# Windowed attention with sinks and a mixing feed-forward layer: rows of two tokens throughout, and a new order of work

## Chip, cores and metric

The kernel runs on one core of a Trainium2 chip. The metric is the device time of one execution in microseconds. Runs come with a state: "fast" runs agree with the fastest of the same kernel within 1.5%, "slow" ones do not and are left out of every ratio. In the kernel before, TensorE's granted clock is 0.98 as a mean over the profiled run.

## The reference, cut to what matters

```python
def _attn_ref(q, k, v, n_sink, window):          # (4, 8, 768, 64) each, n_sink 4, window 128
    scores = scale * np.matmul(q, k.transpose(0, 1, 3, 2))
    keep = is_sink | in_window                   # the first 4 tokens, and the last 128
    a = softmax(np.where(keep, scores, -1e9))    # cut: written out with max, exp, sum
    return np.matmul(a, v)

def _moe_ref(x, mu_k, mu_r, w_k, w_v, w_r):      # x is (4, 768, 512)
    x_prev = ...                                 # x, one token later
    xk = mu_k * x + (1.0 - mu_k) * x_prev
    xr = mu_r * x + (1.0 - mu_r) * x_prev
    k = np.maximum(xk @ w_k, 0.0)                # "keys"
    v = k * k @ w_v                              # "v products"
    r = 1.0 / (1.0 + np.exp(-(xr @ w_r)))        # "gates"
    return r * v
```

## The kernel before: the parts concerned

The work is cut into 12 units of 256 tokens (4 batches, T = 0, 1, 2 in each). A table in the kernel fixes which engine does each movable operation (CHOICE) and the order on each engine (ORDER). Buffers come from pools, and waits follow from what an operation reads and writes. A unit passes through: load; cast to bf16; transpose (on TensorE and evacuated, or by DMA); scores; exponential; mask; values; transpose of x; mix; keys; v products and gates. In the profile lines, `xt` is transposed x, `xk` and `xr` are the mixed x, `rl` the keys after their maximum with 0, `kk` their square, `th` the gates, `ob` an output block, `e` the exponentials, `es` those of the sinks, and `vb` the v rows in bf16.

```python
# evacuation of transposed q and k: pairs of tokens are pulled apart (strided)
copy(out=buf[key][:, 2 * half:2 * half + 2, :, :].rearrange("p c g (t j) -> p c j (g t)", j=2),
     in_=buf[psk].bitcast(BF16)[:, 0:512].rearrange("p (c j t) -> p c j t", c=2, j=2))
...
def scores(c):                                   # 6 products per head pair, 4 of them where T == 0
    jobs = [(kt[:, c, 0, :], 128, 384, qt[:, c, :, :]),
            (kt[:, c, 1, :], 384, 512, qt[:, c, 1, :])]
    if T > 0:
        jobs.append((buf["kt", u - 1][:, c, 1, :], 0, 128, qt[:, c, 0, :]))
...
# mix, for each half of the 512 columns: one subtraction, then a fused multiply-add for each
# of two 128-column blocks and each of xk and xr
nc.vector.tensor_tensor(out=buf[tk], in0=xt[:, c0:c0 + 2, t0:t0 + 256],
                        in1=xt[:, c0:c0 + 2, t0 - 1:t0 + 255], op=ALU.subtract)
nc.vector.scalar_tensor_tensor(
    out=buf[key][:, c0 + i, :], in0=buf[tk][:, i, :],
    scalar=mu[w][:, c0 + i:c0 + i + 1],
    in1=xt[:, c0 + i, t0 - 1:t0 + 255], op0=ALU.mult, op1=ALU.add)
```

The softmax here doesn't subtract the row's maximum and nothing guards it: scores larger than these inputs give would overflow.

## Time and profile before

| | before |
|---|---|
| time, median of 3 runs | 171.59 us (170.52 to 173.14) |
| span of the profiled run | 169.6 us |
| busy TensorE / VectorE / ScalarE / GpSimd | 160.0 / 153.4 / 129.0 / 13.5 us |
| TensorE work, at the smallest spacing of each product | 143.6 us |

The last row is not a row of the page. It is worked out from the trace: each weight load is counted at its start with the spacing of its product as the prediction lists them (216 ns for 512 columns, 109 for 256, and so on; score groups spread over their products). The same count up to a time t says how much TensorE had done by then. I call it "work done".

Beside the lines in the prediction, these are the busy times in three stretches of the kernel before (columns: stretch, length, then busy time and count of PE, PEld, DVE, ACT and POOL, granted clock, DMA share, GB/s; PE is TensorE and PEld its weight loads, DVE is VectorE, ACT ScalarE, POOL GpSimd):

```profile
0.00:30.00 30.00, 24.58 (x231) 15.55 (x231) 23.12 (x66) 21.93 (x34) 5.96 (x22) 0.89 0.97 262
30.00:130.00 100.00, 99.01 (x1041) 66.10 (x1041) 99.26 (x261) 85.61 (x140) 7.51 (x9) 1.00 0.92 214
130.00:176.00 46.00, 36.42 (x335) 24.04 (x332) 31.02 (x78) 21.44 (x36) 0.00 (x0) 0.99 0.35 98
```

In the middle stretch TensorE and VectorE are both full and ScalarE has 14 us of 100 to spare. Over the whole span these shares look much looser (94, 90 and 76%).

### The profile page before, as it was taken

The page shows a single profiled execution, that of the slowest core. Times are in us where ns is not written, and L with a number is a line of the kernel's source. Part 1 is how long each engine was busy: PE and PEld are TensorE (multiplying, and loading weights), DVE is VectorE, ACT ScalarE, POOL GpSimd, SP SyncE. Part 2 cuts the span into 40 slices and gives each one's busy share as a digit, 9 for nine tenths or more (in the row PEclk, how much of TensorE's full clock was granted, in tenths as well). Part 3 has the DMA queues.
Part 4 walks back from the last instruction along what each step waited for, and adds up shares of the span by engine and source line. Part 5 has one row for each costly group of instructions (what it writes and reads, how often), then busy time and mean ns, then how long its engine had stood idle before and what let it go on. Part 6 is the DMA issues. An engine that isn't in the chain of part 4 may idle for free.

```text
span 169.6 us, 4184 instructions
## 1 busy us (share of the span) xinstructions
PE 160.0 (94%) x1602; PEld 105.7 (62%) x1602; DVE 153.4 (90%) x403; ACT 129.0 (76%) x208; POOL 13.5 (8%) x31
## 2 busy tenths in 40 slices
PE   7977879799999999999999999999999999999992
PEld 2544658664657667767567786756476775877551
DVE  6288898999999999999999999999999999799542
ACT  3588797999898999897979986866829849953320
POOL 6330000000200010050000200030000000000000
PEclk9995699999999999999999999999999999999999
DMA  5999989999938979999579489969969858103033
GB/s 142 238 275 320 344 192 326 356 335 276 191 86 214 254 172 231 184 263 287 135 183 221 97 207 225 181 168 233 252 147 266 195 109 233 62 4 124 2 124 124
DMA packets 82803, 33.82 MB, mean 199 GB/s; under 512 B 64736, under 2 KB 77280, under 8 KB 82784
## 3 DMA queue, kind: packets, MB, share of 16 engines
q1 hardware_dynamic: 81728, 33.56, 80.0%
q8 instruction: 12, 0.20, 0.5%
q10 hardware_dynamic: 1056, 0.00, 0.4%
q14 instruction: 7, 0.06, 0.1%
HBM read 24.12 MB, written 6.29 MB: 179 GB/s over the span
## 4 chain that ended last, share of the span: by engine, by line
PE 82%; DVE 10%; DMA 3%; SPq 1%; issue 1%; ACT 0%; POOL 0%; DVEq 0%
PE bank L888 24%; PE bank L839 23%; PE bank L870 12%; PE bank L713 7%; PE sc L654 6%; DMA vs<-in_v_dram 3%; PE bank L752 3%; PE bank L569 2%; PE bank L701 2%; DVE e L690 2%; DVE xk L789 2%; SPq L387 1%; DVE x L729 1%; PE bank L631 1%; PE bank L809 1%
## 5 line engine op out<-in xcount | busy, mean ns | idle before, releaser
L839 PE MATMUL bank<-xk,wk_sb 128*128 128x256 bf16 x384 | 50.5, 273 | 1.1 <-DVE wk_sb L513 0.9
L676 ACT ACTIVATE e<-sc 128x1024 bf16<-128x1024 f32 (+1 forms) x48 | 44.6, 966 | 4.4 <-PE sc L654 4.4
L888 PE MATMUL bank<-wv_h,kk 128*128 128x512 bf16 x184 | 45.8, 379 | 0.0
L839 PEld LDWEIGHTS <-wk_sb 128*128 128x128 bf16 x384 | 35.3, 98 | 9.3 <-DVE wk_sb L513 1.4
L849 ACT ACTIVATE rl<-bank 128x512 bf16<-128x512 f32 x45 | 26.2, 607 | 10.3 <-PE bank L839 7.8
L690 DVE TENSOR_TENSOR e<-e,mask 128x1024 bf16<-128x1024 bf16 (+1 forms) x48 | 30.1, 639 | 0.4 <-POOL ksink L608 0.3
L888 PEld LDWEIGHTS <-kk 128*128 128x128 bf16 x184 | 16.7, 98 | 15.7 <-issue 0.5
L870 PE MATMUL bank<-wr_sb,xr 128*128 128x512 bf16 x96 | 24.2, 379 | 0.0
L789 DVE SCALAR_TENSOR_TENSOR xk<-td,mu,xt 128x256 bf16<-128x256 bf16 x48 | 22.4, 493 | 0.1
L789 DVE SCALAR_TENSOR_TENSOR xr<-td,mu,xt 128x256 bf16<-128x256 bf16 x48 | 22.5, 477 | 0.0
L876 ACT ACTIVATE th<-bank 128x512 f32<-128x512 f32 x24 | 14.8, 620 | 7.8 <-PE bank L870 7.7
L729 DVE TENSOR_TENSOR x<-bank,rec 128x256 bf16<-128x256 f32 x48 | 19.4, 416 | 0.6 <-DVE rec L726 0.3
L897 DVE SCALAR_TENSOR_TENSOR ob<-th,bank 128x512 f32<-128x512 f32 x23 | 15.6, 681 | 4.7 <-ACT th L876 2.6
L861 DVE TENSOR_TENSOR kk<-rl 128x512 bf16<-128x512 bf16 x48 | 19.4, 416 | 0.1
L713 PE MATMUL bank<-vb,e 128*128 128x65 bf16 x352 | 19.2, 195 | 0.2
L713 PEld LDWEIGHTS <-e 128*128 128x128 bf16 x352 | 16.7, 99 | 3.1 <-issue 0.6
L654 PE MATMUL sc<-qt,kt 64*128 64x128 bf16 (+1 forms) x256 | 14.8, 247 | 1.1 <-ACT kt L577 0.7
L870 PEld LDWEIGHTS <-xr 128*128 128x128 bf16 x96 | 8.9, 98 | 8.6 <-issue 0.3
L654 PEld LDWEIGHTS <-kt 64*128 64x128 bf16 x256 | 9.5, 97 | 7.3 <-issue 4.0
L761 ACT COPY xt<-bank 128x512 bf16<-128x512 bf16 x15 | 8.8, 587 | 5.3 <-PE bank L752 4.5
L701 PE MATMUL bank<-vsink,es 128*128 128x130 bf16 x64 | 12.4, 220 | 0.3 <-ACT rl L849 0.3
L779 DVE TENSOR_TENSOR td<-xt 128x512 bf16<-128x512 bf16 x24 | 10.5, 440 | 0.1
(63 smaller groups left out, 163.9 us busy)
## 6 DMA issues: line engine op xcount, KB each, us to landing
vs<-in_v_dram SPq DMA_DIRECT2D x24, 256.0 KB, 4.6
out_dram<-ob SPq DMA_DIRECT2D x23, 256.0 KB, 3.3
ks<-in_k_dram SPq DMA_DIRECT2D x18, 256.0 KB, 4.8
qs<-in_q_dram SPq DMA_DIRECT2D x7, 512.0 KB, 7.3
qs<-in_q_dram SPq DMA_DIRECT2D x10, 256.0 KB, 5.3
w<-in_moe_w_k_dram SPq DMA_DIRECT2D x2, 1024.0 KB, 10.3
w<-in_moe_w_v_dram SPq DMA_DIRECT2D x2, 1024.0 KB, 10.0
ks<-in_k_dram SPq DMA_DIRECT2D x3, 512.0 KB, 8.2
```

What stands on the lines that cost most here:

```text
L654: nc.tensor.matmul(out=sc[:, a, o0:o1], lhsT=lhs[rows], rhs=rhs[rows], start=True, stop=True)
L676: nc.scalar.activation(out=buf[ek][:, :, lo:], in_=buf[sck][:, :, lo:], func=AF.Exp, scale=scale)
L690: nc.vector.tensor_tensor(out=at, in0=at, in1=m, op=ALU.mult)
L701: nc.tensor.matmul(out=o[:, g, :, :], lhsT=buf["es", u][:, 128 * g:128 * g + 128], rhs=vsink[b % 2][:, 2 * c:2 * c + 2, :], start=True, st ...
L713: nc.tensor.matmul(out=o[:, g, a, :], lhsT=e[:, a, e0:e0 + 128], rhs=rhs, start=(T == 0 and i == 0), stop=(i == len(blocks) - 1), skip_gro ...
L729: P.op("DVE", dve(256), lambda ok=ok, rk=rk, c=c: nc.vector.tensor_tensor(out=buf["x", u][:, :, 128 * c:128 * c + 128].rearrange("p g (a d ...
L789: nc.vector.scalar_tensor_tensor(out=buf[key][:, c0 + i, :], in0=buf[tk][:, i, :], scalar=mu[w][:, c0 + i:c0 + i + 1], in1=xt[:, c0 + i, t ...
L839: nc.tensor.matmul(out=ps[:, i, :], lhsT=wk_sb[:, c, 128 * f:128 * f + 128], rhs=xk[:, c, :], start=(c == 0), stop=(c == NC - 1), skip_gro ...
L849: nc.scalar.activation(out=buf[rk], in_=buf[psk].rearrange("p (i t) -> p i t", i=2), func=AF.Relu)
L861: P.op("DVE", dve(512, 0.52), lambda f2=f2, rk=rk: nc.vector.tensor_tensor(out=buf["kk", u][:, 2 * f2:2 * f2 + 2, :], in0=buf[rk], in1=buf ...
L870: nc.tensor.matmul(out=buf[psk], lhsT=buf["xr", u][:, c, 128 * g:128 * g + 128], rhs=wr_sb[:, c, :], start=(c == 0), stop=(c == NC - 1))
L888: nc.tensor.matmul(out=buf[psk], rhs=wv_h[:, f, :], lhsT=buf["kk", u][:, f, 128 * g:128 * g + 128], start=(f == 0), stop=(f == NF - 1))
```

## The change

Its intent: load q, k and v in rows of two consecutive tokens, so that DMA packets are 512 bytes rather than 256; keep tokens in that pair order everywhere, so that the evacuation of q and k is contiguous; move the mix from fused operations to two-source operations and scalings that may go to ScalarE, and some casts to GpSimd; mask the first two units by products added to the scores; and search CHOICE and ORDER anew. Cut to its core:

```diff
 # loads: v like q and k, "h (p j) d -> p h (j d)" with j=2 (two tokens, 512 bytes, in a row)
-                        in_=v[b, :, s0:s0 + 128, :].rearrange("h p d -> p h d")), rank,
+            key, src = (name, u), {"k": k, "q": q, "v": v}[name]
 # casts of q and k: a third engine is allowed
-                       "DVE": (dve(512, 0.52), cast(nc.vector.tensor_copy), True)},
+                       "DVE": (dve(512, 0.52), cast(nc.vector.tensor_copy), True),
+                       "POOL": (590.0, cast(nc.gpsimd.tensor_copy), True)},
 # evacuation: contiguous
-                    out=buf[key][:, 2 * half:2 * half + 2, :, :].rearrange(
-                        "p c g (t j) -> p c j (g t)", j=2),
+                    out=buf[key][:, 2 * half:2 * half + 2, :, :],
 # v rows of two neighbouring units joined (T > 0): two copies of 64 x 1040 per unit
+                P.op("DVE", 456.0, part(nc.vector.tensor_copy), rank, port=True,
+                     alts={"DVE": (456.0, part(nc.vector.tensor_copy), True),
+                           "ACT": (970.0, part(nc.scalar.copy), False)},
 # sinks' v rows: two products with a selection matrix
+            for j in range(2):
+                nc.tensor.matmul(..., lhsT=spread[0:NS // 2, j, :],
+                                 rhs=buf["vb", u][0:NS // 2, j, :, 0:D], start=(j == 0), stop=(j == 1))
 # scores: 8 products of 128 columns per head pair, for every T; exponentials always 1024 wide
+                            out=sc[:, a, :].rearrange("p (j g t) -> p j g t", j=2, g=2)[:, j, g],
+                            lhsT=kt[rows, c, j, at:at + 128], rhs=q2[rows, g],
 # mix: subtract (2 per unit), scale (8), add the shifted tokens (4)
-                        nc.vector.scalar_tensor_tensor(
-                            out=buf[key][:, c0 + i, :], in0=buf[tk][:, i, :],
-                            scalar=mu[w][:, c0 + i:c0 + i + 1],
-                            in1=xt[:, c0 + i, t0 - 1:t0 + 255], op0=ALU.mult, op1=ALU.add)
+                    nc.vector.tensor_scalar(
+                        out=buf[key][:, c, :], in0=buf[xr][:, c, :],
+                        scalar1=mu[w][:, c:c + 1], scalar2=None, op0=ALU.mult)
+                    nc.scalar.activation(out=buf[key][:, c, :], in_=buf[xr][:, c, :],   # or this
+                                         func=AF.Copy, scale=mu[w][:, c:c + 1])
+                    nc.vector.tensor_tensor(out=part, in0=part, in1=behind(g), op=ALU.add)
 # mu: loaded as 8 rows, transposed on TensorE, copied;  CHOICE and ORDER: all new
```

## The prediction

> **What bounds the kernel now.** I read, in this order: the busy table with the slices, the chain that ended last, busy times by window, the timeline of TensorE over the first 30 us, the cost groups by form.
>
> ```profile
> PE 160.0 (94%) x1602; PEld 105.7 (62%) x1602; DVE 153.4 (90%) x403; ACT 129.0 (76%) x208; POOL 13.5 (8%) x31
> ...
> PEclk9995699999999999999999999999999999999999
> ...
> PE 82%; DVE 10%; DMA 3%; SPq 1%; issue 1%; ACT 0%; POOL 0%; DVEq 0%
> ```
>
> TensorE is busy 94% and carries 82% of the chain. VectorE at 90% looks like a second bound, but the windows (columns: length, then busy time and count of PE, PEld, DVE, ACT, POOL, clock, DMA share, GB/s) separate two stages:
>
> ```profile
> 16.00:20.00 4.00, 3.68 (x37) 2.71 (x39) 3.15 (x9) 2.92 (x5) 0.00 (x0) 0.50 1.06 378
> 20.00:24.00 4.00, 2.35 (x20) 1.35 (x16) 4.00 (x10) 4.00 (x6) 0.00 (x0) 0.98 0.83 164
> ...
> 85.00:100.00 15.00, 15.00 (x172) 10.74 (x170) 15.00 (x41) 13.27 (x22) 1.17 (x1) 1.00 0.78 169
> ...
> 145.00:160.00 15.00, 15.00 (x143) 10.90 (x141) 13.24 (x35) 8.31 (x14) 0.00 (x0) 1.00 0.14 54
> ```
>
> After about 30 us TensorE has no holes. "Busy" is modelled, so I also took the spacing of single matmul starts in the trace: 216 ns for 512 columns, 109 for 256, 56 for 128, 29 for the 65-column value products. Everything above these spacings between 30 us and the last matmul (166.1 us) adds up to 3.1 us of 136. VectorE being full there is nearly free of charge. Before 30 us things differ: TensorE at half clock, then short of work while VectorE and ScalarE are full.
>
> ```profile
> 21.54 0.28 PE L631 MATMUL bank<-qt,ksink 128*32 128x256 bf16 x2 [0.79 <-DVE qt L577]
> 21.75 1.05 PE L839 MATMUL bank<-xk,wk_sb 128*128 128x256 bf16 x8
> 22.64 0.59 PE L908 MATMUL bank<-warm 128*128 128x512 bf16 x2
> 24.11 1.92 PE L839 MATMUL bank<-xk,wk_sb 128*128 128x256 bf16 x16 [0.87 <-DVE wk_sb L513]
> ```
>
> The first keys product starts at 21.75 and work is dense only from 24.1 us. From the spacings, all work that is not filling costs: keys 384 x 109 = 41.9 us, v products 184 x 216 + 16 x 109 = 41.4, gates 96 x 216 = 20.7, scores 16 x 0.55 + 8 x 0.44 = 12.3, values 352 x 29 + 64 x 57 = 13.9, transposes 192 x 56 = 10.8, sinks 2.6, sum 143.6 us, plus some 0.1 us at each of 32 switches into the narrower score shapes (a 512-column product before one takes 312, not 216 ns): 146.8 us. At 24.1 us only 6.9 us of it was done. So the time is a start-up of 24 us, a dense TensorE stage of 142, and 3.5 us of tail. Only the start-up and TensorE's own work count.
>
> **What the Trainium skill says.**
> "TensorE: Matmul & The Clock Gate", Part 1 (the HAM clock gate): the array runs at half rate unless it has recently been busy. The trace agrees: clock 0.50 at 16 to 20 us, after holes at 10 to 13, and 1.00 later.
> "VectorE: DVE Perf Modes", What auto-detection actually checks: a two-tensor operation can do two 16-bit results per cycle, a single-source one in SBUF more. The trace agrees for the first: kk (512 elements, two sources) takes 416 ns, while the fused scalar-tensor-tensor takes 477 to 493 for only 256, so it has no fast form here.
> "DMA: Bandwidth & Descriptors", Specifications: line rate wants 512 B or more. The DMA records agree: a 256 B packet takes 20 ns, a 512 B one 30.
> "GPSIMD Engine Reference", Specifications: its SBUF interfaces are shared with VectorE. GpSimd is idle 92% of this run, so this trace cannot show what that costs.
>
> **The change, part by part.** Counts of the changed kernel are from its instruction order.
>
> TensorE. Scores become 16 products of 128 columns per two head pairs for all tokens. Two products on separate row halves start 3 to 4 ns apart and pairs 56 ns apart, so 8 pairs cost about 0.55 us: unchanged where T > 0, +0.11 us for each of 8 groups at T = 0. Values: 352 becomes 384 products, 32 x 29 ns = +0.9 us. The sinks' v rows take two products, not one: 4 x 0.22 = +0.9. A quarter of these falls in the start-up; the dense stage gains about **2.0 us of work** (0.65 + 0.70 + 0.65). The masks of the first two units become 16 added bias products of 512 columns, 3.5 us, all before the first keys product, partly in place of fills (22 become 17).
>
> VectorE. Rows of the groups, mean ns of one at the bar:
>
> ```profile
> L690 DVE TENSOR_TENSOR e<-e,mask 128x1024 bf16<-128x1024 bf16 x32 | 21.3, 681 | 0.2 <-ACT e L676 0.2
> ...
> L779 DVE TENSOR_TENSOR td<-xt 128x512 bf16<-128x512 bf16 x24 | 10.5, 440 | 0.1
> ...
> L577 ACT COPY qt<-bank 128x512 bf16<-128x512 bf16 x11 | 8.3, 757 | 0.2 <-PE bank L569 0.2
> ...
> L591 ACT CAST vb<-vs 128x512 bf16<-128x512 f32 x13 | 8.3, 639 | 0.0
> ```
>
> The mix is 24 subtractions and 96 fused operations, 55.4 us; it becomes 72 two-source operations at 0.44 (31.7) and 45 scalings at an estimated 0.2 us (a four-element reciprocal takes 0.175) = 40.7, so -14.7. Masks: 48 become 40, 30.1 to 27.2. Casts -2.1, eight joins of v rows an estimated +3.6, five more relus +3.4, the rest +1.8. Sum about -11: 142 us.
>
> ScalarE. Evacuations of k and q become contiguous: 17 at 0.745 become 11 at the 0.587 of xt, -6.2. Casts -10.7. Scalings 51 x 0.38 (the 256-element es) = +19.4; eight joins at about 1.04 = +8.3; 16 exponentials grow from 768 to 1024 elements at 0.82 to 1.04, +3.5; others -5.3. Sum +9: 138 us. GpSimd takes 19 casts of q and k and more. Both of VectorE's and ScalarE's totals stay below TensorE's.
>
> DMA. 49,152 packets of 256 B become 24,576 of 512 B: 61.4 to 46.1 us of the 16 engines, share 80 to about 71%. After 40 us no TensorE wait ends on a DMA, so that is free; in the start-up v is 0.64 us per unit cheaper. The mu load (about 1000 packets of 4 B) nearly vanishes, but lies beside other loads.
>
> **Start-up**, where it is decided. ScalarE up to its first cast of wk: now 11.6 us of work from 4.6 us on, so 16.2, really 20.25 (4 us of waits). Then: 6 casts at 0.57, 5 evacuations at 0.55, 2 joins at 1.0, 8 exponentials at 0.97, es and two scalings 1.05: 17.0 us, so 21.6 without waits, and keys from 22.7. VectorE loses eight masks (4.7 us), which made such waits; I allow 1 us and put keys at 23.7. But by then both first units' values and two groups of the third's scores are done, some 8.1 us in the units of before; at 24.1 us that is 8.5 against 6.9: **-1.6 us**. A looser VectorE should save half of the roughly 4 us that were lost after 24 us: **-1.5 to -2**. Against it **+2.0**. If the clock stays up at 13 to 20 us, the chain's TensorE pieces there (3.5 us at half speed) give another 1 us or so. Sum -1 to -3, middle **-2 us**.
>
> **The rivals.**
> A: the start-up gains much more. The new order puts no fill after the first unit's scores, as if TensorE were then always supplied; if so it is dense from about 11 us with 2 us done: 11 + 2.6 of bias + 145 left + 2.8 of switches + 3.5 = 165 us of span, time about 166.5. Against: 17 us of ScalarE work and a DMA share above 1 ahead of wk. The same sort of order in the kernel before lost far more than it planned.
> B: ScalarE becomes the start-up's bound and wk's casts come at 24 to 25 us, or keys of the second unit, which follow at once, wait for its longer mix (subtract, scale, add over two engines, xt still to be evacuated). Then the 2 us of added products come on top: 172 to 173.5.
> C: GpSimd's 20 to 30 us of casts hold VectorE at the shared interface and eat the 11 us. It costs the time only if VectorE falls behind TensorE: 0 to +2 us. For: VectorE's new forms are just those with two SBUF sources or one fast source. Against: casts are few per unit.
>
> **Range and chances.** The middle is 171.6 - 2 = **169.6 us**; A at its best is 166, B and C together 173. I take 166.3 to 172.4. Two per cent faster means below 168.2, which needs most of A: 0.25. Two per cent slower means above 175.0, beyond B: 0.05. Within: 0.70.
>
> **What would show it.** Right: TensorE without holes after about 32 us, VectorE near 142 us and ScalarE near 138, score groups of 16 products at 0.55 us, scalings at 0.2 us on VectorE, first keys product at 23 to 24.5 us with more attention done ahead of it, DMA share near 70%. Wrong: keys near 20 us and clock 1.00 throughout (A); TensorE waiting for xk at 27 to 31 us (B); two-source operations well over 0.44 us beside GpSimd's casts (C); or holes in the later stage, which would mean that a full VectorE had held TensorE in a way that the spacings did not show.

## The result

The changed kernel is correct and takes 178.93 us (median of 4 runs, 177.06 to 179.94), against 172.37 us for the kernel before in the same rounds (4 runs, 170.52 to 173.80). The ratio is **1.0422, 95% interval 1.0342 to 1.0501: slower**. Ratios here are the mean time of one kernel's fast runs over that of the other's fast runs of the same rounds, so not quite the ratio of the medians quoted. One run of the changed kernel (179.94) was slow and is not in the ratio, nor are the two of the kernel before that lie over 1.5% above its fastest (173.14 and 173.80); the profiled one (span 175.3 us) is fast, with clock 1.00.

From the page of the changed kernel: busy times, the granted clock in 40 slices, the largest DMA queue, and the chain that ended last by engine.

```profile
PE 163.2 (93%) x1755; PEld 108.3 (62%) x1778; DVE 149.8 (85%) x413; ACT 141.9 (81%) x236; POOL 36.9 (21%) x81
...
PEclk9999999999999999999999999999999999999999
...
q1 hardware_dynamic: 56880, 33.56, 75.0%
...
PE 31%; ACT 22%; DVE 20%; DMA 9%; SPq 7%; issue 7%; POOL 2%; ACTq 0%; DVEq 0%; POOLq 0%
```

The totals look harmless: TensorE still 93%, VectorE even less busy than before. The chain is what stands out. It was TensorE to 82% in the kernel before; now it wanders between three engines. The same three stretches as above, for the changed kernel, and the 15 us stretch that answers the one shown in the prediction:

```profile
0.00:30.00 30.00, 26.93 (x319) 16.82 (x321) 20.45 (x70) 25.65 (x38) 13.43 (x48) 1.00 1.02 304
30.00:130.00 100.00, 94.76 (x1101) 64.88 (x1115) 95.74 (x258) 95.24 (x162) 23.30 (x32) 1.00 0.94 215
130.00:176.00 46.00, 41.48 (x338) 26.57 (x343) 33.61 (x87) 20.99 (x40) 0.20 (x1) 1.00 0.19 70
...
85.00:100.00 15.00, 14.29 (x163) 9.31 (x162) 14.47 (x41) 14.44 (x27) 3.98 (x7) 1.00 0.77 200
```

In the middle stretch all three engines are at 95%, and none at 99. ScalarE's spare 14 us have shrunk to 5, and TensorE has holes.

"Work done" by TensorE puts numbers to where the time went:

| | before | after | after minus before, as time |
|---|---|---|---|
| done by 30 us | 11.7 | 15.0 | -3.3 |
| done from 30 to 140 us (110 us long) | 106.1 | 99.7 | +6.4 |
| all of it | 143.6 | 146.3 | +2.7 |
| sum | | | +5.8 |

The two spans differ by 175.3 - 169.6 = 5.7 us. So the start-up gained somewhat more than predicted, TensorE got as much more work as counted, and 6.4 us were lost in the stage where TensorE had been dense. The waits of TensorE from 30 to 166 us (engine, line, what it waited for; total us, times, longest), first both of the kernel before, then the four largest of eight in the changed one:

```profile
PE sc L654 <- ACT kt L577: 0.7, 1, 0.7
PE bank L839 <- DVE xk L789: 0.2, 1, 0.2
```

```profile
PE bank L1010 <- DVE ob L1019: 0.9, 1, 0.9
PE bank L992 <- DVE xr L915: 0.8, 1, 0.8
PE bank L961 <- ACT rl L971: 0.8, 1, 0.8
PE bank L711 <- ACT rl L971: 0.6, 1, 0.6
```

The eight waits sum to 4.2 us and end on both side engines (2.6 us on VectorE, 1.6 on ScalarE): there is no single new wait to remove. All of TensorE's idle time from 30 us to its last start, shorter gaps too, is 5.6 us against 1.0; the rest of the 6.4 us is wider spacing of products that the page counts as busy.

The side engines' groups in the changed kernel (busy us, mean ns of one, idle before and what ended it):

```profile
L900 ACT ACTIVATE xr<-xr,mu_all 128x256 bf16<-128x256 bf16 x29 | 14.2, 513 | 1.8 <-DVE xk L895 1.8
L900 ACT ACTIVATE xk<-xr,mu_all 128x256 bf16<-128x256 bf16 x22 | 10.8, 508 | 0.5 <-DVE xr L885 0.3
L664 ACT COPY vj<-vb 64x1040 bf16<-64x1040 bf16 x8 | 8.5, 1057 | 0.2
L895 DVE TENSOR_SCALAR xk<-xr,mu_all 128x256 bf16<-128x256 bf16 x26 | 7.2, 295 | 0.2
L983 DVE TENSOR_TENSOR kk<-rl 128x512 bf16<-128x512 bf16 x48 | 20.7, 440 | 0.0
L648 POOL CAST vb<-vs 128x512 bf16<-128x512 f32 x7 | 6.3, 915 | 24.8 <-DMA vs<-in_v_dram 23.3 <-ACT vj L664 1.5
```

Scalings on ScalarE take 51 x 0.51 us of records; consecutive ones start 399 ns apart, so they fill 20 us of the engine. The same kk rows took 416 ns before; between starts their mean went from 333 to about 360 ns. The mean hides what happened: two of the 48 rows, each beside a GpSimd operation, took 1256 and 678 ns, and the other 46 took 418 in the mean. Taken together, VectorE, ScalarE and GpSimd are busy 153.4 + 129.0 + 13.5 = 295.9 us before and 149.8 + 141.9 + 36.9 = 328.6 us after. The change did not remove side work; it removed some from VectorE and put more of it elsewhere.

### The profile page after: what moved, and what is told of

The parts are those of the page before. It is cut to its first block, busy times and chain, and to the rows that moved or that the text cites.

```text
span 175.3 us, 4603 instructions
## 1 busy us (share of the span) xinstructions
PE 163.2 (93%) x1755; PEld 108.3 (62%) x1778; DVE 149.8 (85%) x413; ACT 141.9 (81%) x236; POOL 36.9 (21%) x81
## 2 busy tenths in 40 slices
DMA packets 56918, 33.86 MB, mean 193 GB/s; under 512 B 14264, under 2 KB 51392, under 8 KB 56896
## 4 chain that ended last, share of the span: by engine, by line
PE 31%; ACT 22%; DVE 20%; DMA 9%; SPq 7%; issue 7%; POOL 2%; ACTq 0%; DVEq 0%; POOLq 0%
PE bank L1010 10%; PE bank L961 9%; ACT e L768 7%; SPq L397 6%; PE bank L992 6%; DMA w<-in_moe_w_k_dram 6%; DVE kk L983 3%; DMA ks<-in_k_dram 3%; DVE x L812 3%; ACT xr L900 2%; DVE e L776 2%; ACT xk L900 2%; ACT vj L664 2%; ACT rl L971 2%; DVE xr L885 2%
## 5 line engine op out<-in xcount | busy, mean ns | idle before, releaser
L768 ACT ACTIVATE e<-sc 128x1024 bf16<-128x1024 f32 x48 | 48.1, 1030 | 0.2 <-PE sc L733 0.2
L1010 PE MATMUL bank<-wv_h,kk 128*128 128x512 bf16 x169 | 44.0, 379 | 1.4 <-DVE ob L1019 0.9
L776 DVE TENSOR_TENSOR e<-e,mask 128x1024 bf16<-128x1024 bf16 x40 | 27.3, 695 | 0.3 <-ACT e L768 0.2
L971 ACT ACTIVATE rl<-bank 128x512 bf16<-128x512 f32 x40 | 23.3, 604 | 5.1 <-PE bank L961 5.1
L900 ACT ACTIVATE xr<-xr,mu_all 128x256 bf16<-128x256 bf16 x29 | 14.2, 513 | 1.8 <-DVE xk L895 1.8
L795 PE MATMUL bank<-vb,e 128*128 128x65 bf16 x256 | 15.3, 193 | 0.4 <-DVE e L776 0.2
L733 PE MATMUL sc<-qt,kt 64*128 64x128 bf16 x384 | 15.0, 217 | 0.1
L864 POOL COPY xt<-xt 128x8 bf16<-128x8 bf16 (+1 forms) x6 | 2.3, 377 | 48.6 <-DVE xt L841 43.0
L885 DVE TENSOR_TENSOR xr<-xt 128x512 bf16<-128x512 bf16 x24 | 10.5, 451 | 1.3 <-ACT xt L841 1.1
L648 POOL CAST vb<-vs 128x512 bf16<-128x512 f32 x7 | 6.3, 915 | 24.8 <-DMA vs<-in_v_dram 23.3
```

What stands on the lines that cost most here:

```text
L733: nc.tensor.matmul(out=sc[:, a, :].rearrange("p (j g t) -> p j g t", j=2, g=2)[:, j, g], lhsT=kt[rows, c, j, at:at + 128], rhs=q2[rows, g] ...
L768: nc.scalar.activation(out=buf[ek], in_=buf[sck], func=AF.Exp, scale=scale)
L776: nc.vector.tensor_tensor(out=buf[ek], in0=buf[ek], op=ALU.mult, in1=m.unsqueeze(1).to_broadcast([128, 2, 512]))
L795: nc.tensor.matmul(out=o[:, g, a, :], lhsT=e[:, a, j, g, :], rhs=vv[:, j, 2 * c + a, :], start=(T == 0 and j == 0), stop=(j == 1), skip_gr ...
L900: nc.scalar.activation(out=buf[key][:, c, :], in_=buf[xr][:, c, :], func=AF.Copy, scale=mu[w][:, c:c + 1])
L971: nc.scalar.activation(out=buf[rk], in_=buf[psk].rearrange("p (i t) -> p i t", i=2), func=AF.Relu)
```

## The experiments

The theory, called J in the expectations: the side engines are **jointly** too full from 30 to 130 us. They hand work to one another (exponential on ScalarE, mask on VectorE; subtract on VectorE, scale on ScalarE, add on VectorE), so with both at 95% each waits for the other and TensorE for both. Rivals: one engine alone is the bound (ScalarE by its scalings, or VectorE, or GpSimd through what it shares with VectorE), or the new order is at fault, not the load (O). Several kernels give wrong results, where an operation was shortened; they have the same number of instructions and the same order.

### Shorten one load at a time

ScalarE's scalings cut to 112 columns (wrong result). The expectation says 38 of the 51; the run's trace has 45 of 112 columns and 6 of 256, so 45 were cut, here and in the later runs that contain this cut:

```diff
-                    nc.scalar.activation(out=buf[key][:, c, :], in_=buf[xr][:, c, :],
+                    n = 256 if w == 0 and u < 4 else 112
+                    nc.scalar.activation(out=buf[key][:, c, 0:n], in_=buf[xr][:, c, 0:n],
```

> Changed kernel, wrong results on purpose: 38 of ScalarE's 51 scalings cover 112 of 256 columns, so that one should take about the 280 ns that the kernel's plan assumes and not the 400 ns between starts that its trace shows. Theory S (from 30 to 130 us ScalarE is the bound, because its scalings cost more than planned): 38 x 0.12 = 4.6 us less ScalarE work, the time falls by 3 to 5 us against the changed kernel, to some 174 to 176. Theory V (VectorE is the bound) and theory G (GpSimd's casts hold VectorE): under 1 us. Theory P (added TensorE work and the start-up): none.

VectorE's 40 masks halved (wrong):

```diff
-                nc.vector.tensor_tensor(out=buf[ek], in0=buf[ek], op=ALU.mult,
-                                        in1=m.unsqueeze(1).to_broadcast([128, 2, 512]))
+                nc.vector.tensor_tensor(out=buf[ek][:, 0:1], in0=buf[ek][:, 0:1], op=ALU.mult,
+                                        in1=m.unsqueeze(1))
```

> Changed kernel, wrong results on purpose: all 40 mask multiplications of VectorE cover one head's half (512 of 1024 columns), some 0.60 to 0.33 us each, so 10 to 11 us less VectorE work. Theory S: VectorE only waits for ScalarE, the time falls by less than 2 us. Theory V: it falls by 5 us or more, more than in the first run. If both engines limit in turn, about half of what is taken away comes back in each of these two runs.

GpSimd's casts of q, k and v, 22 of them, cut to 32 columns (wrong):

```diff
-                       "POOL": (590.0, cast(nc.gpsimd.tensor_copy), True)},
+                       "POOL": (590.0, cast_short if u > 2 else cast(nc.gpsimd.tensor_copy), True)},
```

> Changed kernel, wrong results on purpose: from the fourth unit on GpSimd's casts of q, k and v copy 32 of 512 columns, so that GpSimd hardly uses the SBUF interface that it shares with VectorE in the dense stage (some 22 casts of 0.7 to 0.9 us). Theory G: VectorE's two-source operations return to their uncontended spacing (kk 0.371 to 0.335 us on average between starts) and the time falls by 3 us or more. Theories S and V: 0 to 1.5 us (VectorE gets 2 to 3 us back).

| run | this, median | before, median | ratio, 95% interval | span |
|---|---|---|---|---|
| e1_short_scal_act | 176.32 us | 170.65 us | 1.0364, 1.0285 to 1.0443 | 174.4 us |
| e2_half_masks_dve | 176.33 us | 170.65 us | 1.0333, 1.0287 to 1.0379 | 174.7 us |
| e3_short_gpsimd_casts | 175.51 us | 170.65 us | 1.0301, 1.0230 to 1.0371 | 174.1 us |

Against the 1.0422 of the unaltered change these are 0.6 to 1.2% less each, and the intervals overlap that of the change (1.0342 to 1.0501), so each by itself is weak evidence. What they do say is that none of these loads makes the loss by itself: ScalarE lost 4.9 us of busy time (a quarter of what its scalings take), VectorE 8.2 and GpSimd 11.8, and most of the loss stayed each time. Work done from 30 to 140 us is 101.0, 100.5 and 101.7 us, against 99.7. With GpSimd's casts short, the kk rows are back at 416 ns:

```profile
L989 DVE TENSOR_TENSOR kk<-rl 128x512 bf16<-128x512 bf16 x48 | 19.5, 416 | 0.0
```

The same shows in all of VectorE's operations. In the changed kernel, from 30 to 140 us, 13 of them last over 100 ns more than the median of their group (same line, tiles and shape), every one while a GpSimd operation runs, 4.5 us in all. In the kernel before these are 3 and 1.1 us, with short casts 3 and 0.9 us. So single VectorE operations become much longer beside GpSimd, which is rival C of the prediction. The whole run gains 1.2%, uncertain by about as much.

### All three at once

> Changed kernel, wrong results on purpose: the cuts of the first three runs together (38 ScalarE scalings at 112 columns, all masks halved, GpSimd's later casts at 32 columns), with the order kept. Alone they gave some 1, 1.5 and 2 us. Theory J (ScalarE, VectorE and GpSimd limit the dense stage jointly, by their load): more than the sum, 5 to 7 us against the changed kernel, some 171 to 173, with TensorE's holes after 30 us back to 2 or 3 us. Theory O (the order was made for durations that are not the real ones, so that engines wait for each other in turn): about the sum of the three, 3 to 5 us.

172.82 us against 171.51 us, ratio 1.0094 (1.0017 to 1.0170), span 171.1 us. Three cuts that return 0.6, 0.9 and 1.2% singly return 3.3% together, about 5.6 us. This interval lies well apart from the change's. That it is more than the sum of the three (2.7%) is not clear of the noise, so J's "more than the sum" is not shown. The middle stretch:

```profile
30.00:130.00 100.00, 97.08 (x1140) 66.84 (x1155) 88.49 (x267) 95.61 (x170) 10.64 (x32) 1.00 0.94 218
```

VectorE has fallen from 95.7 to 88.5, ScalarE stays at 95.6 as more of the work falls into the stretch, TensorE is back from 94.8 to 97.1, and 104.2 us of work are done from 30 to 140 us. The instructions and their order are those of the change; only lengths differ. So the new layout's dependences and TensorE's own new products, all still there, can't be the main cause, nor can the order by itself, whatever the load. This run does not rule out theory O as written: the plan had assumed shorter operations (a scaling of 280 ns, for one), the cuts bring some of them near to that, and O's 3 to 5 us lie within the noise of 5.6. The run with a new order, below, is the test of O.

### Short joins, and all four

The copies that join v rows, 12 of 16 cut from 1040 to 64 columns (wrong):

```diff
+                    n = 1040 if u < 3 else 64
-                        out=buf[vj][...].rearrange("p j h d -> p (j h d)"),
-                        in_=buf["vb", w][...].rearrange("p j h d -> p (j h d)"))
+                        out=buf[vj][...].rearrange("p j h d -> p (j h d)")[:, 0:n],
+                        in_=buf["vb", w][...].rearrange("p j h d -> p (j h d)")[:, 0:n])
```

> Changed kernel, wrong results on purpose: 12 of the 16 joins of v rows (six on ScalarE, six on VectorE) copy 64 of 1040 columns, some 0.8 us of ScalarE and 0.3 us of VectorE less each, 6.6 us in all. Theory L (the joins, an extra cost of the rows of two tokens, make the loss): 4 us faster or more. Theories O and J: about 1 to 2 us, like the other single cuts.

177.07 us against 171.51, ratio 1.0339 (1.0270 to 1.0407); its profiled span, 175.5 us, is that of the change. Nothing can be read from it alone beyond "little". On top of the other three:

> The changed kernel with all four cuts of side work: e5_all_three_short and the short joins of v rows of e7_short_joins on top (wrong results on purpose). Theory J (side engines jointly too full between 30 and 130 us): TensorE is then fed as in the kernel before in that stage, ScalarE in 30 to 130 us below 88 us, and the time comes near the kernel before, 171 to 172.5 us, ratio 0.998 to 1.008; it doesn't go much below, since TensorE itself has 2.7 us more to do and the start-up lead is 3.3 us. A floor of TensorE's own (the new products or their switches cost more than the spacings show) would leave it at e5's 172.8 us whatever the side engines do.

172.94 us against 171.44, ratio 1.0103 (1.0036 to 1.0169): no better than without, which is the outcome written down for a floor of TensorE's own. ScalarE is at 92.3 of 100 us, not below 88 as I expected, and work done from 30 to 140 us is 104.1 us, still 2 below the kernel before. A smaller part of the loss (2 us of it) is thus left when all four loads are short. Shortened operations still pay their start, and ScalarE still has 171 of them in that stretch where the kernel before has 140. Part of the 2 us is TensorE's own, as the trace shows. Each pair of products for the sinks' v rows takes 0.64 us with the steps into and out of it (from one v product's start at 44.62 us to the next at 45.47 are 852 ns, less 216 for the v product), where the single product of the kernel before takes 0.22 (75.78 to 76.21 us: 435 ns, less 216). The work count gives a pair 0.43, so three pairs after 30 us hide some 0.6 us of the 2. What keeps the other 1.4 us is open.

### The other way round: load the kernel before

The strongest test leaves the change out. To the kernel before, idle work was added that nobody reads; results stay right, layout and planned order are untouched. That order was not planned for the added work, so this tests load added to a fixed order.

```diff
+                if 3 <= u <= 9:      # behind each exponential: 28 scalings of 256 columns on ScalarE
+                    nc.scalar.activation(out=dum_a, in_=mask.rearrange("p k q -> p (k q)"),
+                                         func=AF.Copy, scale=mu[0][:, 0:1])
...
+                    if u > 2:        # beside each cast of v: 18 casts of 128x512 on GpSimd
+                        nc.gpsimd.tensor_copy(out=dum_g, in_=buf["v", u][:, g, :, :])
```

> The kernel before, with 28 idle ScalarE scalings of 256 columns added behind the exponentials of units 3 to 9 (nobody reads them; the result stays right): about 11 us of ScalarE work of the kind that the change brought, all of it beside the dense stage. Theory J: ScalarE goes from 86 to about 96 us in 30 to 130 us while VectorE stays full, TensorE loses work there, the time rises by 1.5 to 3.5 us, ratio 1.009 to 1.02. If slack on ScalarE in that stage is free (the view that the prediction took, totals below TensorE's), within 0.3%.

> The kernel before, with 18 idle GpSimd casts of 128x512 from float32 added beside the casts of v from unit 3 on (nobody reads them; the result stays right): about 15 us of GpSimd work as in the changed kernel. If VectorE pays for GpSimd through the memory port that they share, VectorE's two-source operations (kk 332 ns between starts) become 5 to 10% longer beside them, and with VectorE the full engine the time rises by 1 to 2.5 us, ratio 1.006 to 1.015. If sharing is harmless, within 0.3%.

> Both additions to the kernel before. Theory J: the loads add up or more, +3 to +6 us, ratio 1.018 to 1.035, and the windows look like those of the changed kernel (TensorE 95, VectorE and ScalarE each 95 or more of 100 us). If the loss of the changed kernel comes from its other order of work or its new dependences rather than from load, well under 2 us.

| run | this, median | ratio, 95% interval | span | work done 30 to 140 us |
|---|---|---|---|---|
| before | 171.44 us | 1 | 169.6 us | 106.1 us |
| e10_before_more_act | 176.03 us | 1.0289, 1.0209 to 1.0368 | 174.7 us | 101.1 us |
| e11_before_more_gpsimd | 174.50 us | 1.0165, 1.0055 to 1.0274 | 173.3 us | 103.4 us |
| e12_before_more_both | 176.02 us | 1.0260, 1.0168 to 1.0351 | 174.1 us | 102.2 us |

From the first of these, the added group and the middle stretch; then the kk rows and the added casts of the second:

```profile
L681 ACT ACTIVATE dum_a<-mask,mu 128x256 bf16<-128x256 bf16 x28 | 14.5, 518 | 0.0
...
30.00:130.00 100.00, 96.17 (x985) 63.09 (x984) 96.27 (x250) 91.85 (x162) 6.95 (x9) 1.00 0.85 203
```

```profile
L867 DVE TENSOR_TENSOR kk<-rl 128x512 bf16<-128x512 bf16 x48 | 20.2, 432 | 0.1
L596 POOL CAST dum_g<-vs 128x512 bf16<-128x512 f32 x18 | 16.4, 912 | 61.0 <-DMA vs<-in_v_dram 60.8
```

Ten microseconds of ScalarE work (busy 129.0 to 138.9 us over the span) cost the kernel before about 5 us, more than I had put down, although ScalarE is then only 92% busy in the middle stretch. The loss of work done, 5.0 us, comes near the change's 6.4. The route is mostly direct. These are TensorE's four longest waits from 30 to 166 us:

```profile
PE bank L843 <- ACT qt L579: 0.7, 1, 0.7
PE sc L656 <- ACT kt L579: 0.7, 1, 0.7
PE bank L892 <- ACT rl L853: 0.6, 1, 0.6
PE bank L892 <- ACT th L880: 0.3, 1, 0.3
```

Of the ten listed, eight end on ScalarE (3.2 us: evacuations, casts, maxima, gates) and two on VectorE (0.4). ScalarE's spare 14% were thus what let it come in time. VectorE falls from 99.3 to 96.3 in those 100 us with nothing added to it: its waits there, 0.4 us before, are 3.0 us, 1.6 of them for TensorE and 1.4 for ScalarE. GpSimd's casts cost 1.65% (an interval of a per cent each way), with kk at 432 ns; they also read the loaded v and may hold its buffer longer, which was not separated. The two do not add: both together cost no more than ScalarE's alone. J as I had written it for this run ("add up or more") is wrong in that; its windows (TensorE 97.3, VectorE 98.4, ScalarE 91.2 of 100 us) do not look like the change's either. That ScalarE's load alone costs the dense stage 5.0 us of work done, and GpSimd's 2.7, is shown.

### Move the scalings, or the order

All 51 scalings of ScalarE to VectorE (CHOICE and ORDER only; correct):

> Changed kernel, right results: all of ScalarE's 51 scalings go to VectorE at their planned places in time; ScalarE loses 51 x 0.40 = 20 us, VectorE gains 51 x 0.196 = 10 us. Theory S with slack on VectorE: 3 us faster or more. Theory V or both engines near full: VectorE is now over full from 30 to 130 us, the time is the same or up to 5 us longer, and VectorE's idle time in that stage shrinks to below 1 us per 100.

184.95 us against 170.65, ratio 1.0825 (1.0749 to 1.0901), span 183.4 us, the worst of all: VectorE is at 98.0 of 100 us from 30 to 130, and 51 x 0.2 us moved to it cost about 8 us of span. That is more than the 5 us written down for a full VectorE, and its idle time, 2.0 us, did not fall below 1. At these places in the order, giving all scalings back to VectorE is no remedy.

The same engines with the order searched anew, using measured durations as costs (correct):

> Changed kernel, right results, every operation on the same engine as in the changed kernel, so each engine has the same work; only the order on each engine is searched anew with the measured durations. Theory O: most of what the re-planned kernel gains, 4 to 6 us. Theory J (load): under 1.5 us, all the gain of the re-planned kernel is then from the choice of engines.

177.11 us against 171.51, ratio 1.0361 (1.0265 to 1.0457), span 175.2 us. Its interval holds the change's 1.0422: the order is worth about 0.6%, not clear of zero and short of O's 4 to 6 us. By stage it is worth more: 101.9 us of work are done from 30 to 140 us (the change: 99.7), but only 13.0 by 30 us (15.0), so this order gains 2.2 us in the dense stage and pays them in the start-up.

Engines and order both searched anew with measured durations (scalings on ScalarE 51 to 35, joins on ScalarE 8 to 3, q and k casts on GpSimd 18 to 12; correct):

> Changed kernel, right results, every operation the same; only the choice of engine and the order on each engine are searched anew with the durations that this case's trace shows between starts (scaling on ScalarE 400 ns instead of 280, casts on GpSimd 720 to 780 instead of 590 to 760, a weight cast there 2000 instead of 1060, the edge copy there 390 instead of 130). ScalarE's scalings 51 become 35, its joins 8 become 3. Theory O or S: 4 to 7 us faster than the changed kernel, about level with the kernel before. Theory J by load alone or theory P (added TensorE work): under 2 us.

175.26 us against 171.51, ratio 1.0251 (1.0166 to 1.0337). This is the best correct version with the new layout; it is still slower than the kernel before, and no run beat that one. Sharing the load better, with its own order, gives back about 1.7% of the 4.2, 2.9 us, between what O and S (4 to 7) and J (under 2) had said. No correct version was found that gives back the rest.

## Why the prediction was wrong

**The bound, read from the trace before: right as far as it went.** TensorE was dense and VectorE full in the middle stage, and the spacings lost little there. The inference from it was wrong: "VectorE being full there is nearly free of charge" and "Both of VectorE's and ScalarE's totals stay below TensorE's" treat each side engine as a budget over the whole span.

**The step that failed:** "A looser VectorE should save half of the roughly 4 us that were lost after 24 us: -1.5 to -2." In place of a gain of 1.5 to 2 us the dense stage lost 6.4 us of work. Two things were wrong in this step.

First, the 4 us were not there to be saved. By the prediction's own sums 146.8 - 6.9 = 139.9 us of work stood in the 142 us after 24.1 us, which leaves about 2. Most of the rest must be the score switches, which these sums had already counted as work. TensorE's idle time from 24.1 us to its last start is only 1.3 us in the kernel before.

Second, a VectorE and a ScalarE with totals below TensorE's do not keep TensorE supplied. The kernel before with ScalarE at 138.9 us (predicted for the change: 138) and VectorE as full as ever is 2.9% slower. The changed kernel with the first three cuts has both engines below their predicted totals (VectorE 137.9 of 142, ScalarE 136.4 of 138) and is still 0.9% slower than the kernel before where 1.2% faster was predicted, with 104.2 us of work done from 30 to 140 us and not over 106.1. So the step fails at the predicted sizes too. The other 3.3% go with the loads that these cuts took away, and the loads above the predicted sizes are the next point.

**Sizes.** ScalarE came out at 141.9 us, predicted 138. Its scalings were put at 0.38 us after the 256-element es, and take 0.51; 51 x 0.13 = 6.6 us. The es row has a constant scale and the scaling takes its scale from memory, one value per partition. The Trainium skill states just this in "ScalarE: Activation LUTs", section What ACT_TABLE_LOAD costs: 186 ns + 0.833 ns per element with immediate scale and bias, about 93 ns more for each per-partition operand, and about 93 ns of overlap between neighbours. For 256 elements these figures give an estimate of 492 ns, and 399 between starts; the trace shows 508 to 513, and 399. I had that page and did not use it. VectorE came out at 149.8, predicted 142: scalings 0.30 us in the records (196 ns between starts, which is the 0.2 of the estimate), and single operations longer beside GpSimd (4.5 us from 30 to 140 us).

**TensorE's own work: nearly right.** Score groups take 0.55 us; the counted work grew by 2.7 us, of which the prediction put three quarters, 2.0, in the dense stage. Too low was the second product for the sinks' v rows, put at 0.22 us: with its steps in and out it adds 0.42, some 0.6 us more for the three pairs after 30 us.

**Start-up: right in kind, put somewhat too small.** The first keys product starts at 23.20 us, predicted 23.7, with the second unit's values and scores of the third done ahead of it:

```profile
22.05 0.28 PE L795 MATMUL bank<-vb,e 128*128 128x65 bf16 x4
22.27 0.62 PE L733 MATMUL sc<-qt,kt 64*128 64x128 bf16 x16
22.82 0.40 PE L836 MATMUL bank<-ident,x 128*128 128x128 bf16 x4
23.20 0.61 PE L961 MATMUL bank<-xk,wk_sb 128*128 128x256 bf16 x4
```

The clock is 1.00 throughout. Predicted: 1.6 us ahead at 24.1 us and 1 more from the clock. Measured: 9.9 - 6.9 = 3.0 us ahead at 24.1 us, 3.3 at 30 us. Had the dense stage kept its density, -3.3 + 2.7 would have left the time within 1 us of the kernel before.

**DMA:** the packets fell from 82,803 to 56,918 and the largest queue's share from 80.0 to 75.0% (predicted 71; the 256-byte packets that are left take 27 ns in the mean, not 20). No wait of TensorE after 30 us ends on a DMA, as said; what the layout alone is worth was not tested.

**Rivals.** A named the clock and a larger start-up gain, and both came, smaller than in A. B did not happen. C is real and is part of it: 1.2% for the change, 1.65% for the kernel before with casts added, the latter 2.8 us in the middle of its interval, above C's "0 to +2 us". The prediction's last sentence named holes in the later stage as what would prove it wrong, but gave that no number and 5% for anything slower by 2%. Open stay most of the 2 us that all four cuts leave, why the two added loads do not add, and how far an order planned for the real loads could absorb them.

## What to carry to other kernels

In this kernel the spare share of ScalarE in the dense stage was a cushion and not a budget. Where two engines are full and a third feeds both, count added side work in the stage where it runs, and ask who will wait for it. Ask too whether what a change is to save is there: sum the idle time of the bounding engine first. Before making such a change, try it cheaply: add idle work of the same kind to the kernel as it is, which here lost 5.0 us of work in the dense stage where the change lost 6.4. And look up an operation's operand kinds before borrowing another operation's duration.

## What the Trainium skill lacked or had wrong

- "GPSIMD Engine Reference", Specifications, names the interfaces that GpSimd and VectorE share, but that row gives no size (other pages on it were not used here). Here, with GpSimd 21% busy, 13 VectorE operations from 30 to 140 us became over 100 ns longer while a GpSimd operation ran, one of them 1256 ns instead of 418, 4.5 us in all; with short casts 3, 0.9 us in all. 18 added casts of 128x512 cost the kernel before 1.65%.
- I found no page that says what the spare time of a side engine is worth when two others are full. Here 28 scalings of 399 ns on an engine that was 86% busy in that stage cost 2.9% of the time.
